# Pairing heads 4 to 7 as (5,4) and (7,6) from the second group on

## The chip, the cores and the metric

The kernel runs on one core of a Trainium2 chip. A core has five engines that run their own instruction streams side by side: PE (TensorE, matrix products; its weight loads are listed apart as PEld), DVE (VectorE), ACT (ScalarE), POOL (GpSimd) and SP (SyncE, which here only issues DMA transfers). Data moves between DRAM and the on-chip memory by 16 DMA engines; a transfer is issued by an instruction on SP, ACT or POOL and lands later. The on-chip memory has 128 partitions; a tile lies across them, and an instruction works on all the partitions of a tile, or on a part of them, at once.

The metric is the device time of one execution in microseconds (us). The kernel before takes 655.81 us, the median of 3 runs (653.32 to 656.08).

## The reference

An attention with decay over 4 batches, 8 heads, 768 positions and head size 64, whose output, with heads side by side, is the 3072x512 input x of two matrix products with a pointwise function between them:

```python
q, k, v: (4, 8, 768, 64) float32; lam: (8,) in 0.97 to 0.99
w_in: (512, 2048); w_out: (2048, 512)          # both float64
for b in range(nb):                            # blocks of 64 positions
    qb, kb, vb = (q[:, :, sl], k[:, :, sl], v[:, :, sl])
    intra = np.einsum('bhic,bhjc->bhij', qb, kb) * Dmask[None]
    intra = np.einsum('bhij,bhjd->bhid', intra, vb)
    inter = np.einsum('bhid,bhde->bhie', qb * lam_pow[None], kv_state)
    out[:, :, sl] = intra + inter
    kv_state = lam_block * kv_state + einsum(kb * rev_pow, vb)
x = np.ascontiguousarray(out.transpose(0, 2, 1, 3)).reshape(B * S, H * D)
h = x @ w_in
g = h - np.tanh(h)
return (g @ w_out).astype(np.float32)
```

The row index of w_in is head times 64 plus the place in the head. The order in which the kernel keeps the 512 values of a token is therefore free, as long as the rows of w_in are in the same order.

## The kernel before

**Tiling.** The kernel takes blocks of 128 positions. A group g (0 to 5) is one such block of all 4 batches: 512 tokens, of which half 0 is batches 0 and 1 (P0) and half 1 batches 2 and 3 (P1). For each group the attention gives x transposed (`xt`: 4 chunks of 128 rows, 256 tokens a half), the first product gives the hidden values, the second the output. Products after group 0 are made by sums and seven products of half size in place of eight (`up`, L640), the second product from group 1 on by two levels of this (`down_twice`, L932). The summed blocks of w_out lie in DRAM (`fine`) and are fetched again for every group through POOL's queue into a ring of seven buffers named `wb` (L814). A matmul that finds its `wb` block not landed waits.

**Heads in pairs.** The 8 heads are handled as four pairs p of two heads j, one in partitions 0 to 63 and one in 64 to 127. Before, pair p holds heads 2p and 2p+1 in this order. The scores of a pair are masked by powers of lam (`mask0` in group 0, `mask` from group 1 on, both made at the start), and the state is kept in `state`, two heads of a pair one below the other. `fwd` (`powers`) holds lam's powers for q, one row per place in the pair.

**x is written in a swapped order.** From group 1 on a tile of scores is shared by the pairs p and p+2, pair p with one half of the positions in the upper rows and pair p+2 with the other, and `out_banks` puts the output of pairs 2 and 3 into the opposite half of the partitions (`1 - j`). So the rows of x come as heads 0, 1, 2, 3, 5, 4, 7, 6. w_in must be in the same order: its blocks m = 0 and 1 of a unit (512 columns; there are four units) come in one transfer to 128 partitions each, the blocks m = 2 and 3 in two transfers to 64 partitions each, to swapped halves (`load_block`, L238). The raw 64-bit weights are rounded to float32 by three ACT copies (L318 to L320) and two DVE operations (L322, L323) a block, with four raw buffers (`WAHEAD`), so that block n+4 is not issued until block n has been rounded.

**Loads of q, k and v.** Everything here is issued by SP in the order in which the program states it. In groups 0 and 1, q and k come in natural layout (L156), are transposed on PE (L374) and copied out of PSUM by ACT (`att_transpose`, L376, one copy of 128x512 for q and one for k). From group 2 on, q and k come as blocks: `load_blocks` fetches them, one tile for q and one for k of each batch, with four transfers a tile (L174), each to 32 partitions with pieces of up to 1 KB for four heads; DVE then turns the tile in 32x32 squares (L352). The natural k and v (L161, three transfers each) are needed as well, for the state and the output. `load(n)` is called by the first user of a group's blocks and issues the whole group from group 2 on: k and v of batches, the blocks of batches 0 to 3, and the natural k and v that remain; a block's transfer must wait until the tile that it goes into has been turned. SP's transfers use eight completion semaphores in turn, and an issue waits until the transfer eight before it has landed.

**Order at the start.** SP issues q, k and v of batches 0 and 1, then q and k of batch 2, w_in blocks 0 and 1, q and k of batch 3, w_in block 2, v of batches 2 and 3, and w_in block 3. PE does group 0's attention for batches 0 and 1, begins the first product of unit 0 (`up_plain`, L1012) between the parts for batches 2 and 3, whose `state_products` (L421) needs their v, and then goes on with w_in block by block. Group 1's transposes follow while the rest of the weights arrives.

**Order later.** Tile's scheduler places what isn't tied (`keep_in_program_order`); matmuls of the attention for the next group are put between the products of the current one. `out_late` (L508) and `out_early` (L522) multiply v with the masked scores, `score_products` (L458) k with q. `copy_xt` (L412) brings x out of PSUM.

Of the kernel before, what the change touches and what calls it, by code (L numbers as in the profile page):

```python
# [24 lines left out]
def kernel(  # L25
# [79 lines left out]

    mask = const.tile([128, 4, 3, HF], F32)

    def masks():
        inj = work.tile([128, BLK], F32, name="inj", tag="qd")
        cross = work.tile([128, 4, 2, HF], F32, name="cross", tag="qd")  # L110
        lo, hi = ts(0, HF), ts(1, HF)
        nc.gpsimd.memset(inj[hi, HF:BLK], 0.0)
        nc.gpsimd.tensor_copy(inj[hi, 0:HF], ident[hi, HF:BLK])
        for n in range(4):
            tc.keep_in_program_order(nc.vector.tensor_tensor_scan(
                out=cross[hi, n].rearrange("s c i -> s (c i)"), data0=lam_all[hi, n + 4:n + 5].to_broadcast([HF, BLK]),
                data1=inj[hi], initial=0.0, op0=AL.mult, op1=AL.add))
        m0 = mask0.rearrange("s j p (c i) -> s p j c i", c=2)
        for q in range(2):
            n = ts(q, 2)  # L120
            nc.gpsimd.tensor_copy(mask[lo, n, 0:2], m0[lo, q])
            nc.gpsimd.tensor_copy(mask[lo, n, 2], m0[lo, q + 2, :, 0])
            nc.gpsimd.tensor_copy(mask[hi, n, 1], m0[hi, q, :, 1])
        nc.gpsimd.tensor_copy(mask[hi, :, 0:3:2], cross[hi])

    fwd = const.tile([128, NP, BLK], F32)

    def powers():
        for j in range(2):
            tc.keep_in_program_order(nc.vector.tensor_copy(  # L130
                fwd[ts(j, 64), :, 0], lam_all.rearrange("s (p j) -> s j p", j=2)[ts(j, 64), j, :]))
        m = 1
        while m < BLK:
            tc.keep_in_program_order(nc.vector.tensor_tensor(
                fwd[:, :, m:2 * m], fwd[:, :, 0:m], fwd[:, :, m - 1:m].to_broadcast([128, NP, m]), op=AL.mult))
            m *= 2
# [3 lines left out]
    bwd = [mask[:, :, c, HF - 1:HF].to_broadcast([128, H // 2, D]) for c in (1, 2)]  # L140
# [23 lines left out]
    def load_blocks(g, b, names):  # L164


        for name, src in (("q", q), ("k", k)):
            if name in names:
                x = late["blk"].tile([128, NP, 4 * D], F32, name=f"{name}_blk", tag="blk")
                for c in range(4):  # L170
                    n = 4 * D - 32 * (c % 2)
                    at_ = src[b, c // 2, g * BLK, 32 * (c % 2):]
                    rows = bass.AP(tensor=at_.tensor, offset=at_.offset, ap=[[4 * D, 32], [2 * S * D, NP], [1, n]])
                    tc.keep_in_program_order(nc.sync.dma_start(out=x[ts(c, 32), :, 0:n], in_=rows))  # L174
# [55 lines left out]
    def load_block(eng, dst, kind, n, m, first=False):  # L230
# [3 lines left out]
        elif m < 2:  # L234
            tied(first, eng.dma_start(out=dst, in_=w_in_u[ts(m, 128), n]))
        else:
            for j in range(2):
                tied(first, eng.dma_start(out=dst[ts(1 - j, 64)], in_=w_in_u[ts(2 * m + j, 64), n]))  # L238
# [123 lines left out]
    def att_transpose(g, bs):  # L362
        for b in bs:
# [4 lines left out]
            for dst, x in ((qt, "q"), (kt, "k")):  # L368
                if g >= GB:
                    turn_block(dst, t[x + "b"])  # L370
                else:
# [4 lines left out]
                    tied(True, nc.scalar.activation(dst, tp, AF.Copy))  # L376
# [28 lines left out]
    def out_banks():  # L405
        ops = [bank("op", "att", 4).rearrange("d (p b s) -> d p b s", p=2, b=2) for _ in range(2)]
        return ops, lambda n, p, j: ops[p // 2][ts(j if p < 2 else 1 - j, 64), p % 2, n, :]
# [7 lines left out]
    def state_products(g, bs, kv):  # L415
        kv = kv.rearrange("d (b p e) -> d b p e", b=2, p=NP)
        for n, b in enumerate(bs):
            kd, vn = raw[g, b]["k"], raw[g, b]["v"]
            for p in range(NP):
                for j in range(2):  # L420
                    tied(True, nc.tensor.matmul(out=kv[ts(j, 64), n, p, :], lhsT=kd[:, 2 * p + j, :],  # L421
                                                rhs=vn[:, 2 * p + j, :], start=n == 0 and p == 0, stop=True,
# [7 lines left out]
    def first_out(bs):  # L430
        ops, dst = out_banks()
# [51 lines left out]
    def att_read(g, bs):  # L483
        half = bs[0] // 2
        begun = (g, half) in outs
        if not begun:
            outs[g, half] = out_banks()
# [12 lines left out]
    def out_late(g, bs, first=False):  # L500
        if first:
            outs[g, bs[0] // 2] = out_banks()
        _, dst = outs[g, bs[0] // 2]
        for n, b in enumerate(bs):
            ss, vn = sc[g, b], raw[g, b]["v"]
            for p in range(NP):
                for j in range(2):
                    tied(True, nc.tensor.matmul(out=dst(n, p, j)[:, HF:BLK], lhsT=vn[:, 2 * p + j, :],  # L508
# [4 lines left out]
    def out_early(g, bs):  # L513
        ops, dst = outs.pop((g, bs[0] // 2))
        behind = seen.pop((g, bs[0] // 2), None)
        for n, b in enumerate(bs):
            ss, vn = sc.pop((g, b)), raw[g, b]["v"]
            for q in range(2):
                for p in (q, q + 2):
                    for j in range(2):  # L520
                        r = ts(p // 2, HF)
                        mm = tied(True, nc.tensor.matmul(out=dst(n, p, j)[:, 0:HF], lhsT=vn[r, 2 * p + j, :],  # L522
# [836 lines left out]
```

## Time and profile before

| | us |
|---|---|
| median of 3 runs | 655.81 (653.32 to 656.08) |
| the profiled execution | 655.09 |
| its span | 653.3 |
| granted PE clock | 1.000 |
| DVE, ACT, POOL busy | 494.7, 241.1, 231.0 |
| moved by DMA | 140.45 MB, mean 215 GB/s |
| SP's and ACT's transfers (hardware queues) | 28.0% of 16 engines' span |
| POOL's transfers (software queue) | 46.9% of it |

The span goes from the first instruction that is recorded to the last; the time of the execution holds 1.8 us besides. The two largest groups of POOL's transfers are the `wb` fetches and the writes of `fine`:

```profile
L814 POOL DMA_DIRECT2D wb<-fine x217 | 116.7, 539 | 219.8 <-PE y L932 110.5 <-PE y L867 38.5 <-PE zw L932 30.8
L305 POOL DMA_DIRECT2D fine<-f x32 | 20.9, 658 | 3.6 <-DMA fine<-f 1.4 <-DVE ws L323 0.9 <-DVE ws L285 0.4
```

A line of this kind reads: source line, engine, operation, what it writes and reads, how many; then the busy time in us and the mean in ns of one; then the idle time of that engine just before them and what ended most of it. The groups that turn the q and k blocks, on DVE:

```profile
L352 DVE STREAM_TRANSPOSE kt<-k_blk 128x512 f32<-128x512 f32 x16 | 17.8, 1110 | 0.0
L352 DVE STREAM_TRANSPOSE qt<-q_blk 128x512 f32<-128x512 f32 x16 | 17.7, 1107 | 0.0
```

The share of DMA in a row of windows is that of the busy time of 16 engines, and it may be above 1 where records overlap. In a row in order of time the first number is the time from the span's start, the second the length, and a bracket holds the idle time before and what ended it.

### The profile page before, as it was taken

What the parts mean: (1) busy time and instruction counts of PE and PEld (TensorE: products, weight loads), DVE (VectorE), ACT (ScalarE), POOL (GpSimd) and SP (SyncE); (2) the same over time, 40 slices, a digit from 0 to 9 for tenths busy, and PEclk for the clock granted to TensorE, in tenths of its full rate; (3) what the DMA queues carried; (4) which work ended last, traced back from release to release, by engine and by line L of the source; (5) the groups of instructions that cost most, each with busy time, mean ns of one, the idle gap of its engine ahead of it and who ended that gap; (6) DMA issues with size and microseconds to landing.
All of it is one profiled execution on the core that took longest, in us unless ns stands there. A gap on an engine that the chain in (4) does not pass through costs nothing.

```text
span 653.3 us, 14777 instructions
## 1 busy us (share of the span) xinstructions
PE 639.9 (98%) x5792; PEld 589.3 (90%) x5792; DVE 494.7 (76%) x884; ACT 241.1 (37%) x484; POOL 231.0 (35%) x396
## 2 busy tenths in 40 slices
PE   7899999999999999999999999999999999999998
PEld 6688888888888999988999988999988999988997
DVE  4798997996876976898768777878777878256583
ACT  3788682603321223442122453222344212444110
POOL 2120247773113554243455100546201356300450
PEclk9999999999999999999999999999999999999999
DMA  9979978999458876999978775779693587610582
GB/s 215 223 204 187 281 235 296 327 317 290 114 157 221 261 228 221 250 286 239 296 244 287 202 145 130 234 241 303 200 195 98 161 290 252 213 39 0 158 280 80
DMA packets 108261, 140.45 MB, mean 215 GB/s; under 512 B 64032, under 2 KB 81568, under 8 KB 108192
## 3 DMA queue, kind: packets, MB, share of 16 engines
q0 software_dynamic: 29840, 97.54, 46.9%
q1 hardware_dynamic: 78208, 41.96, 28.0%
q8 instruction: 46, 0.75, 0.5%
q14 instruction: 23, 0.19, 0.1%
q10 hardware_dynamic: 144, 0.00, 0.0%
HBM read 117.18 MB, written 23.86 MB: 216 GB/s over the span
## 4 chain that ended last, share of the span: by engine, by line
PE 72%; DMA 4%; DVE 3%; issue 3%; POOL 2%; ACT 1%; POOLq 0%; DVEq 0%; ACTq 0%
PE y L640 17%; PE y L932 14%; PE zw L932 11%; PE z L640 6%; PE w L640 5%; PE y L738 4%; DMA wb<-fine 3%; PE z L738 2%; PE acc L1042 2%; PE y L867 2%; PE sp L458 2%; DMA fine<-f 1%; PE op L508 1%; POOL wb L814 1%; PE op L494 1%
## 5 line engine op out<-in xcount | busy, mean ns | idle before, releaser
L814 POOL DMA_DIRECT2D wb<-fine x217 | 116.7, 539 | 219.8 <-PE y L932 110.5
L932 PE MATMUL y<-wb,g 128*128 128x128 f32 x624 | 81.4, 276 | 1.3 <-DMA wb<-fine 1.3
L935 ACT ACTIVATE q<-y 128x128 f32<-128x128 f32 x108 | 29.9, 277 | 137.9 <-PE y L932 137.9
L932 PEld LDWEIGHTS y<-wb,g 128*128 128x128 f32 x624 | 75.3, 192 | 2.3 <-DVE q L890 1.4
L932 PE MATMUL zw<-wb,g 128*128 128x128 f32 x416 | 55.3, 276 | 0.8 <-DMA wb<-fine 0.7
L932 PEld LDWEIGHTS zw<-wb,g 128*128 128x128 f32 x416 | 50.6, 192 | 1.3 <-issue 0.5
L640 PE MATMUL y<-xt,w 128*128 128x256 f32 x200 | 46.9, 380 | 0.0
L648 ACT ACTIVATE th<-g 128x512 f32<-128x512 f32 x42 | 26.5, 630 | 51.9 <-DVE g L671 20.0
L1012 PE MATMUL h<-xt,w 128*128 128x256 f32 x192 | 44.2, 382 | 1.0 <-DVE w L323 1.0
L653 DVE TENSOR_TENSOR g<-g,th 128x512 f32<-128x512 f32 x42 | 29.1, 692 | 17.4 <-ACT th L648 17.2
L640 PEld LDWEIGHTS y<-xt,w 128*128 128x128 f32 x200 | 37.6, 190 | 5.1 <-ACT g L680 0.2
L1012 PEld LDWEIGHTS h<-xt,w 128*128 128x128 f32 x192 | 35.7, 190 | 6.4 <-DVE w L323 0.9
L640 PE MATMUL w<-xt,w 128*128 128x256 f32 x168 | 40.4, 382 | 0.0
L640 PE MATMUL z<-xt,ws 128*128 128x256 f32 x168 | 39.7, 379 | 0.0
L640 PE MATMUL y<-tt,w 128*128 128x256 f32 x160 | 38.1, 381 | 0.0
L640 PE MATMUL y<-tt,ws 128*128 128x256 f32 x160 | 38.1, 380 | 0.0
L640 PEld LDWEIGHTS z<-xt,ws 128*128 128x128 f32 x168 | 31.9, 190 | 4.3
L640 PEld LDWEIGHTS w<-xt,w 128*128 128x128 f32 x168 | 31.0, 190 | 4.5 <-ACT w L611 0.4
L640 PEld LDWEIGHTS y<-tt,w 128*128 128x128 f32 x160 | 30.1, 190 | 4.3
L932 PE MATMUL y<-wb,s 128*128 128x128 f32 x248 | 32.8, 275 | 1.0 <-DMA wb<-fine 1.0
L640 PEld LDWEIGHTS y<-tt,ws 128*128 128x128 f32 x160 | 30.0, 190 | 3.9
L932 PE MATMUL zw<-wb,s 128*128 128x128 f32 x248 | 32.8, 275 | 0.0
(216 smaller groups left out, 1373.9 us busy)
## 6 DMA issues: line engine op xcount, KB each, us to landing
wb<-fine POOLq DMA_DIRECT2D x217, 256.0 KB, 3.8
fine<-f POOLq DMA_DIRECT2D x24, 256.0 KB, 4.9
wb<-fine_in POOLq DMA_DIRECT2D x24, 256.0 KB, 4.3
raw<-in_moe_w_out_dram POOLq DMA_DIRECT2D x10, 512.0 KB, 6.6
raw<-in_moe_w_in_dram SPq DMA_DIRECT2D x8, 512.0 KB, 5.2
raw<-in_moe_w_in_dram SPq DMA_DIRECT2D x16, 256.0 KB, 6.0
q_blk<-in_q_dram SPq DMA_DIRECT2D x32, 128.0 KB, 4.2
k_blk<-in_k_dram SPq DMA_DIRECT2D x32, 128.0 KB, 5.0
```

The source lines that it names most:

```text
L458: tied(True, nc.tensor.matmul(out=dst, lhsT=keys(p, j, late_), rhs=qt[ts(j, 64), p, rows], start=True, stop=True))
L494: tied(True, nc.tensor.matmul(out=dst(n, pp, j), lhsT=state[r, b, pp, :], rhs=tr[g, b][2][r, pp, :], start=not begun and n == 0 and p == 0 ...
L640: tied(g == 0, nc.tensor.matmul(out=t[:, m, :], lhsT=wt[:, kt, ts(m, 128)], rhs=x[:, kt, :], start=first and m == 0 and kt == 0, stop=kt = ...
L648: tied(g == 0, nc.scalar.activation(th, src, AF.Tanh))
L653: tied(g == 0 or g >= GI and inside, nc.vector.tensor_tensor(dst(c), src, th, op=AL.subtract))
L738: tied(True, nc.tensor.matmul(out=dst[:, ts(u, 128)], lhsT=a, rhs=b, start=x in (1, 2, 5) and u == 0, stop=True, skip_group_check=True))
L814: nc.gpsimd.dma_start(out=t.rearrange("p m c -> p (m c)"), in_=fine[TWICE.index(n_), SLOT.index(x_)].rearrange("p u c -> p (u c)"))
L867: nc.tensor.matmul(out=t[:, m, :], lhsT=a[:, u, kt, ts(m, 128)], rhs=wb[:, kt, :], start=first and u == 0 and m == 0 and kt == 0, stop=u = ...
L932: tied(True, nc.tensor.matmul(out=dst, lhsT=a[:, u, :], rhs=wb[:, ts(u, 128)], start=x in begins and u == 0, stop=u == NU - 1, skip_group_ ...
L935: nc.scalar.activation(keep, dst, AF.Copy)
L1012: tied(u == 0 or u == 2 and cs[0] == 11, nc.tensor.matmul(out=hm[c][:, m, :], lhsT=w1[u][:, i, a, ts(m, 128)], rhs=xt[0, t][:, i, :], star ...
L1042: nc.tensor.matmul(out=acc[n][:, r, :], lhsT=a[:, ts(r, 128)], rhs=b, start=kt == 0 and r == 0, stop=kt == KH - 1, skip_group_check=True)
```

## The change

A function `head(p, j)` names the head in place j of pair p: as before for pairs 0 and 1, and swapped, (5,4) and (7,6), for pairs 2 and 3. Because `out_banks` swaps those pairs again, x comes in natural order. Group 0 keeps natural pairs in its scores and writes its output unswapped (`out_banks(0)`), while its state products already use the swapped pairing. All that reads or writes a head by its pair follows: `powers` (four copies in place of two), `masks` (two copies more on POOL, and two into the new constant `fall`, which holds the decay of the lower half and which DVE's decay now reads in place of a slice of the mask), the slices of k and v in `state_products`, `out_late` and `out_early`. In group 1, whose transposes on PE are as before, ACT's copy out of PSUM is made as three: pairs 0 and 1 at once, and two of 64 partitions that swap the halves of pairs 2 and 3. The q and k blocks from group 2 on, whose transfers took four heads at a constant step, now take two heads each, so a tile has eight transfers in place of four. Every w_in block is one transfer.

Instructions on each engine, before and after, without the semaphore and register kinds: PE 2930 and 2930, in the same sequence; DVE 886 and 888; ACT 487 and 503; POOL 401 and 405; SP 290 and 410.

```diff
+    def head(p, j):
+        return 2 * p + (j if p < 2 else 1 - j)
...
     mask = const.tile([128, 4, 3, HF], F32)
+    fall = const.tile([128, 4], F32)
...
         for n in range(4):
+            h = head(n // 2 + 2, n % 2)
             tc.keep_in_program_order(nc.vector.tensor_tensor_scan(
-                out=cross[hi, n].rearrange("s c i -> s (c i)"), data0=lam_all[hi, n + 4:n + 5].to_broadcast([HF, BLK]),
+                out=cross[hi, n].rearrange("s c i -> s (c i)"), data0=lam_all[hi, h:h + 1].to_broadcast([HF, BLK]),
                 data1=inj[hi], initial=0.0, op0=AL.mult, op1=AL.add))
...
             nc.gpsimd.tensor_copy(mask[lo, n, 0:2], m0[lo, q])
-            nc.gpsimd.tensor_copy(mask[lo, n, 2], m0[lo, q + 2, :, 0])
+            for j in range(2):
+                nc.gpsimd.tensor_copy(mask[lo, 2 * q + j, 2], m0[lo, q + 2, 1 - j, 0])
             nc.gpsimd.tensor_copy(mask[hi, n, 1], m0[hi, q, :, 1])
         nc.gpsimd.tensor_copy(mask[hi, :, 0:3:2], cross[hi])
+        for j in range(2):
+            nc.gpsimd.tensor_copy(fall[:, j::2], mask[:, 1 - j::2, 2, HF - 1])
...
         for j in range(2):
-            tc.keep_in_program_order(nc.vector.tensor_copy(
-                fwd[ts(j, 64), :, 0], lam_all.rearrange("s (p j) -> s j p", j=2)[ts(j, 64), j, :]))
+            for p in (0, 2):
+                h = head(p, j)
+                tc.keep_in_program_order(nc.vector.tensor_copy(
+                    fwd[ts(j, 64), p:p + 2, 0], lam_all[ts(j, 64), h:h + 3:2]))
         m = 1
...
     bwd0 = mask0.rearrange("s j p i -> s p j i")[:, :, :, BLK - 1:BLK].to_broadcast([128, NP, 2, D])
-    bwd = [mask[:, :, c, HF - 1:HF].to_broadcast([128, H // 2, D]) for c in (1, 2)]
+    bwd = [x.to_broadcast([128, H // 2, D]) for x in (mask[:, :, 1, HF - 1:HF], fall[:, :, None])]
...
                     n = 4 * D - 32 * (c % 2)
-                    at_ = src[b, c // 2, g * BLK, 32 * (c % 2):]
-                    rows = bass.AP(tensor=at_.tensor, offset=at_.offset, ap=[[4 * D, 32], [2 * S * D, NP], [1, n]])
-                    tc.keep_in_program_order(nc.sync.dma_start(out=x[ts(c, 32), :, 0:n], in_=rows))
+                    for p in (0, 2):
+                        at_ = src[b, head(p, c // 2), g * BLK, 32 * (c % 2):]
+                        rows = bass.AP(tensor=at_.tensor, offset=at_.offset, ap=[[4 * D, 32], [2 * S * D, 2], [1, n]])
+                        tc.keep_in_program_order(nc.sync.dma_start(out=x[ts(c, 32), p:p + 2, 0:n], in_=rows))
                 raw[g, b][name + "b"] = x
...
             tied(n > 4, eng.dma_start(out=dst, in_=moe_w_out[ts(2 * (n + m) - n % 2, 128), :].rearrange("k (a n) -> k a n", a=2)))
-        elif m < 2:
+        else:
             tied(first, eng.dma_start(out=dst, in_=w_in_u[ts(m, 128), n]))
-        else:
-            for j in range(2):
-                tied(first, eng.dma_start(out=dst[ts(1 - j, 64)], in_=w_in_u[ts(2 * m + j, 64), n]))
...
                                                                    identity=ident))
-                    tied(True, nc.scalar.activation(dst, tp, AF.Copy))
+                    if g == 0:
+                        tied(True, nc.scalar.activation(dst, tp, AF.Copy))
+                        continue
+                    tied(True, nc.scalar.activation(dst[:, 0:2], tp[:, 0:2], AF.Copy))
+                    for j in range(2):
+                        tied(True, nc.scalar.activation(dst[ts(j, 64), 2:4], tp[ts(1 - j, 64), 2:4], AF.Copy))
             tr[g, b] = [qt, kt, None]
...
-    def out_banks():
+    def out_banks(g):
         ops = [bank("op", "att", 4).rearrange("d (p b s) -> d p b s", p=2, b=2) for _ in range(2)]
-        return ops, lambda n, p, j: ops[p // 2][ts(j if p < 2 else 1 - j, 64), p % 2, n, :]
+        return ops, lambda n, p, j: ops[p // 2][ts(j if p < 2 or g == 0 else 1 - j, 64), p % 2, n, :]
...
                 for j in range(2):
-                    tied(True, nc.tensor.matmul(out=kv[ts(j, 64), n, p, :], lhsT=kd[:, 2 * p + j, :],
-                                                rhs=vn[:, 2 * p + j, :], start=n == 0 and p == 0, stop=True,
+                    tied(True, nc.tensor.matmul(out=kv[ts(j, 64), n, p, :], lhsT=kd[:, head(p, j), :],
+                                                rhs=vn[:, head(p, j), :], start=n == 0 and p == 0, stop=True,
                                                 skip_group_check=True))
...
     def first_out(bs):
-        ops, dst = out_banks()
+        ops, dst = out_banks(0)
         for n, b in enumerate(bs):
...
         if not begun:
-            outs[g, half] = out_banks()
+            outs[g, half] = out_banks(g)
         ops, dst = outs[g, half]
...
         if first:
-            outs[g, bs[0] // 2] = out_banks()
+            outs[g, bs[0] // 2] = out_banks(g)
         _, dst = outs[g, bs[0] // 2]
...
                 for j in range(2):
-                    tied(True, nc.tensor.matmul(out=dst(n, p, j)[:, HF:BLK], lhsT=vn[:, 2 * p + j, :],
+                    tied(True, nc.tensor.matmul(out=dst(n, p, j)[:, HF:BLK], lhsT=vn[:, head(p, j), :],
                                                 rhs=ss[:, j, p % 2, 1 + p // 2, :], start=first and n == 0 and p % 2 == 0,
...
                         r = ts(p // 2, HF)
-                        mm = tied(True, nc.tensor.matmul(out=dst(n, p, j)[:, 0:HF], lhsT=vn[r, 2 * p + j, :],
+                        mm = tied(True, nc.tensor.matmul(out=dst(n, p, j)[:, 0:HF], lhsT=vn[r, head(p, j), :],
                                                          rhs=ss[r, j, q, 0, :], start=False, stop=True,
```

## The prediction

> **What bounds the kernel now.** I read the busy shares first, then busy time by ten-microsecond window, then the order of time on PE, SP and ACT in the windows where PE is not full, and last the landing of single transfers. First the page's busy line and the chain that ended last:
>
> ```profile
> PE 639.9 (98%) x5792; PEld 589.3 (90%) x5792; DVE 494.7 (76%) x884; ACT 241.1 (37%) x484; POOL 231.0 (35%) x396
> ...
> PE 72%; DMA 4%; DVE 3%; issue 3%; POOL 2%; ACT 1%; POOLq 0%; DVEq 0%; ACTq 0%
> ```
>
> PE is busy for 639.9 of 653.3 us. All that any change of transfers and copies can win is therefore the 13.4 us in which PE idles. The windows (columns: window, its length, busy PE, PEld, DVE, ACT, POOL with counts, clock, DMA share, GB/s) say where these are:
>
> ```profile
> 10.00:20.00 10.00, 8.82 (x121) 7.63 (x121) 5.46 (x11) 7.06 (x13) 0.00 (x0) 1.00 1.18 260
> 20.00:30.00 10.00, 8.57 (x100) 7.07 (x99) 7.34 (x21) 5.57 (x10) 0.58 (x1) 1.00 1.05 237
> 30.00:40.00 10.00, 9.51 (x44) 8.05 (x43) 8.83 (x11) 8.97 (x16) 6.34 (x5) 1.00 0.78 218
> 300.00:310.00 10.00, 9.05 (x120) 8.58 (x112) 9.11 (x17) 2.79 (x7) 4.29 (x8) 1.00 1.02 244
> 310.00:320.00 10.00, 8.39 (x71) 8.10 (x72) 6.40 (x10) 1.39 (x5) 4.00 (x8) 1.00 0.92 304
> ```
>
> Some 5.9 us are lost before 40 us, 2.6 us in 300 to 320, about 1.6 us in four small places between 110 and 230, and 3 us behind the last matmul. Everywhere else PE is full, at clock 1.00. Of the early loss, these three waits stand behind a w_in block (PE in order of time):
>
> ```profile
> 24.16 0.69 PE L421 MATMUL kv<-v_nat,k_nat 128*64 128x64 f32 x16 [0.23 <-DMA v_nat<-in_v_dram]
> 26.04 0.69 PE L421 MATMUL kv<-v_nat,k_nat 128*64 128x64 f32 x16 [1.19 <-DMA v_nat<-in_v_dram]
> 30.89 8.04 PE L1012 MATMUL h<-xt,w 128*128 128x256 f32 x36 [0.49 <-DVE w L323]
> ```
>
> Together 1.91 us. The other early waits are for the first q, k and POOL's identity, ahead of any block that changes.
>
> **Part 1, w_in blocks in one transfer.** Eight blocks (m of 2 and 3, four units) lose one of two issues each, 8 issues of some 0.59 us in all. The issues cost nothing by themselves: SP has slack. What counts is how fast the bytes land, since DMA is full here (share 1.05 to 1.18) and v_nat of batches 2 and 3 stands behind block 2:
>
> ```profile
> 12.21 4.08 SPq L238 DMA_DIRECT2D raw<-in_moe_w_in_dram  x2
> 16.34 1.21 SPq L156 DMA_DIRECT2D v_nat<-in_v_dram  x2
> 17.59 5.28 SPq L238 DMA_DIRECT2D raw<-in_moe_w_in_dram  x2
> ```
>
> Windows of one microsecond, in the same columns, show the rate while a whole block lands (13 to 14) and while the two halves of block 2 land (20 to 23):
>
> ```profile
> 13.00:14.00 1.00, 1.00 (x22) 0.93 (x19) 0.69 (x2) 0.51 (x1) 0.00 (x0) 1.00 1.00 401
> 20.00:21.00 1.00, 1.00 (x7) 0.59 (x7) 1.00 (x2) 0.79 (x2) 0.00 (x0) 1.00 1.27 124
> 22.00:23.00 1.00, 1.00 (x7) 0.90 (x6) 0.96 (x2) 0.00 (x0) 0.00 (x0) 1.00 0.94 155
> ```
>
> Landing by landing: whole blocks 0 and 1 land 1.28 and 1.39 us behind what went before; the pair of block 2 takes 3.79 us (19.26 to 23.05), the pair of block 3 1.80 us (25.91 to 27.71). So one block saves between 0.5 us (1.80 - 1.3) and 2.5 us (3.79 - 1.3). With 1.5 us, the middle, v_nat of batch 3 lands at 24.4 instead of 25.91 and block 3 two savings earlier: all three waits close. With 0.5 us about 1.0 of the 1.91 us close. I take 1.7 us of gain, bounds 1.0 and 1.9. It carries on because behind 30.89 PE, ACT and DVE wait for each other and no longer for w_in (PE is 10.00 of 10 us from 40 to 110).
>
> **Part 2, ACT's copies in group 1.** Eight copies of 128x512 (600 ns each, L376) become one 128x256 and two 64x256 each, 16 instructions more. No 256-wide copy is in the trace; between 277 ns (128x128, L935) and 600 ns it comes to 385 ns, 1155 for three. By durations that is +0.56 us a tile, 4.4 us in all; by the start-to-start step of copies in a row (0.48 against 0.60 us, so 0.12 overlaps) +0.3 us a tile, 2.5 us in all. They lie at 59.8, 70.6 and 74.9 us, and ACT then waits anyway (idle in the brackets):
>
> ```profile
> 70.12 0.60 ACT L1019 ACTIVATE th<-h 128x512 f32<-128x512 f32 x1 [1.72 <-PE h L1012]
> 74.89 0.60 ACT L376 ACTIVATE qt<-tp 128x512 f32<-128x512 f32 x1 [1.33 <-PE tp L374]
> 81.89 1.08 ACT L412 ACTIVATE xt<-op 128x512 f32<-128x512 f32 x2 [2.51 <-PE op L522]
> ```
>
> Queued behind the copies are the w_out conversions, which DVE's L323 waits for; DVE slips by some 0.7 us at 73 and 78 us and regains it in its own waits for ACT (0.35 at 84.86, 0.41 at 86.66). PE needs the results of this stretch from 93.6 us on. Price 0; without that cover, up to 1.3 us.
>
> **Part 3, small work.** Two more copies of `powers` on DVE (the two there take 0.34 us together) and four on POOL (64x64 and 128x2; the row for 64x64 is 0.23 us) lie before 30.4 us; POOL's sums end at 36.5 and PE reads them from 43.16. PE's matmuls keep number, order and shape, only slices change; DVE's decay reads `fall` instead of the mask. Price 0, at most 0.3 us.
>
> **Part 4, the q and k blocks in twice the transfers.** 128 issues become 256 of half the size: each group from 2 on has 8 tiles (q and k of four batches), and a tile has 8 issues instead of 4. One issue lasts 0.43 us (median of L174), so a tile takes SP 3.4 us instead of 1.7. SP also uses eight completion semaphores in turn: the second piece of q for batch 3 is issued at 267.69, right when the eighth before it (261.26, landing 6.4 us later) has landed. Eight in flight are now one tile, not two. Behind the blocks on SP stand the natural k and v:
>
> ```profile
> 265.12 4.04 SPq L174 DMA_DIRECT2D q_blk<-in_q_dram  x4
> ...
> 273.44 5.17 SPq L161 DMA_DIRECT2D k_nat<-in_k_dram  x3
> ...
> 282.77 2.33 SPq L161 DMA_DIRECT2D v_nat<-in_v_dram  x3
> ```
>
> The last piece of v for batch 1 lands at 291.2; PE needs it at 296.9 (L508), 295.2 with the gain of part 1. From 260.9 on, four tiles take four rounds of landing time L; then 12 issues of 0.62 us and a landing of about 4 us: in time while 260.9 + 4L + 11.4 < 295.2, L < 5.7 us. Before, with twice the bytes in flight, L was 6.4 to 9.7 us for most of these; DMA is full there (share 1.12), so with half the bytes in flight I take about half, 4.1 to 4.5: no wait. The blocks' own users (DVE L352) have more: q of batch 2 lands by some 269 and is turned at 273.4. Groups 4 and 5 have L of 3 to 5.6 and 5 us or more to spare. In group 2 each tile's issue waits for a DVE turn every 5.5 us: hidden.
>
> Behind that, blocks for group 4 are issued from about 298 us to 314 instead of 296.7 to 306.5. At 310.3, 311.8 and 313.9 PE waits 1.28, 0.31 and 0.96 us for wb; these transfers share DMA with the blocks (12 pieces, 1.4 MB, land from 304 to 314). At 0.47 us an issue the halves bring 1.2 MB in that time: -0.3 us, bounds -2.5 (stall gone) and +1.5 (it moves behind 314). In group 4 the same overlap arises for the first time, from 409.8, when wb starts again (needed 4.9 us after issue, 2.9 to 3.5 now): +0.2, bounds 0 and 1.
>
> A rule of the Trainium skill speaks against part 4: the page "DMA: Bandwidth & Descriptors", section "Measured", puts a 64 KB transfer at 0.95 us and calls smaller ones descriptor-dominated. By it, as an estimate, 32 halves would take 30 us and v would be late by about 7.5 us, some 661.5 us in all. The trace does not bear it out: 64 KB pieces of v (388.7 to 389.7 us) land 0.4 to 0.5 us apart.
>
> **Sum.** -1.7 + 0 + 0 + (-0.3 + 0.2) = -1.8 us. The profiled execution took 655.09 us (653.3 span, 1.8 around it), which gives 653.3; the median of the runs, 655.81, lies 0.7 us above it, so 654.0.
>
> **Rivals.** (A) The forecast: 654.0, own range 652.5 to 655.6.
> (B) Slower: v_nat of group 3 comes late. It decides from L = 5.7 us. If a half keeps 7.2 us (landing set by POOL's traffic, not by SP's own bytes in flight), v is 4 x 1.5 = 6 us late at L508, a full PE stall: 660.0. For it: the first block at 260.9 took 4.2 us with nothing of SP's ahead, the second 6.4. Against: that traffic eases by 294 (share 0.89).
> (C) Faster: the wb stall at 310 goes as well, since SP feeds its blocks more thinly: 655.81 - 1.7 - 2.55 = 651.6. For it: DMA share 1.04 to 1.13 from 304 to 314. Against: the blocks come later and so stay longer.
> (D) Whole blocks land no earlier, the 124 GB/s at 20 us being DMA's mix and not the halves: 655.8. Against it: 401 GB/s at 13 us at the same share.
>
> **How the numbers follow.** A 0.52, B 0.15, C 0.22, D 0.11. What a measurement here can tell from no change is 0.5%, 3.3 us: below 652.5 and above 659.1. Faster: C and the edge of A, 0.25; slower: B, 0.15; same: 0.60. The range runs from 651.2 to 658.3: A, D, most of C and the mild part of B.
>
> **What would show it.** Right: no v_nat wait at L421 near 24 to 26 us; block 2 landing 1.3 us behind k; PE some 1.7 us earlier at 40 and still at 290; L508 of group 3 unwaited. Wrong: a DMA wait at L508 or L458 near 295, block landings over 5.7 us, longer wb waits at 310 or 410, or ACT's copies delaying L1042.

## The result, and the profile after

The changed kernel takes 661.44 us (median of 7 runs, 658.11 to 662.49) where the kernel before takes 653.35 (7 runs, 652.86 to 656.97). The ratio is 1.0101, with a 95% interval of 1.0074 to 1.0127: 1% slower, 6.6 us by the ratio, where 1.8 us faster (654.0), with a range up to 658.3, had been forecast. Beside the last experiments the changed kernel was run again: 659.57 us, ratio 1.0071 (1.0046 to 1.0096). The profiled execution of the first seven took 658.11 us, the shortest of them, with a span of 656.3, 3.0 us more than that of before.

The page's busy line and the chain that ended last:

```profile
PE 642.1 (98%) x5792; PEld 590.2 (90%) x5792; DVE 494.4 (75%) x886; ACT 245.6 (37%) x500; POOL 232.3 (35%) x400
...
PE 68%; DMA 6%; SPq 4%; DVE 3%; issue 2%; POOL 2%; ACT 1%; DVEq 0%; POOLq 0%; ACTq 0%
```

PE's sequence of matmuls has not changed, and yet PE counts as busy for 2.2 us longer. SPq, SP's own issuing, stands in the chain with 4%; before it was not there. The windows of the changed kernel, in the columns used in the prediction:

```profile
10.00:20.00 10.00, 8.81 (x121) 7.73 (x122) 5.41 (x11) 7.01 (x13) 0.00 (x0) 1.00 1.17 289
20.00:30.00 10.00, 8.94 (x101) 7.15 (x101) 8.58 (x24) 7.70 (x14) 1.66 (x3) 1.00 0.83 268
30.00:40.00 10.00, 10.00 (x48) 8.79 (x47) 9.15 (x13) 7.25 (x13) 6.04 (x5) 1.00 0.70 218
...
300.00:310.00 10.00, 9.44 (x83) 9.21 (x81) 8.36 (x15) 1.99 (x6) 5.37 (x10) 1.00 0.88 248
310.00:320.00 10.00, 7.90 (x61) 7.07 (x60) 6.22 (x11) 1.39 (x5) 3.80 (x8) 1.00 1.06 286
320.00:330.00 10.00, 9.54 (x79) 8.89 (x78) 8.09 (x12) 1.39 (x5) 5.04 (x10) 1.00 0.98 301
400.00:410.00 10.00, 10.00 (x197) 9.09 (x196) 6.84 (x11) 3.39 (x7) 0.48 (x1) 1.00 0.46 122
410.00:420.00 10.00, 8.66 (x74) 8.11 (x72) 8.76 (x14) 1.39 (x5) 5.43 (x11) 1.00 0.95 239
```

Up to 40 us PE idles less than before, from 310 on more, and at 410 there is a hole that was not there. Before, these were the rows for 400 to 420 us:

```profile
400.00:410.00 10.00, 10.00 (x195) 9.06 (x194) 6.89 (x11) 3.39 (x7) 0.24 (x1) 1.00 0.24 47
410.00:420.00 10.00, 10.00 (x92) 10.00 (x91) 8.55 (x14) 1.66 (x6) 6.08 (x12) 1.00 0.76 248
```

Since both kernels run the same 5,792 matmuls in the same order, the sharpest view is to take the start of each matmul in the one trace from its start in the other (negative: the changed kernel is ahead):

| at (time in before) | changed minus before, us | step |
|---|---|---|
| 24 | -0.2 | |
| 26 | -1.59 | v of batch 3 is early |
| 31 to 114 | -1.14 | 0.45 given back at once |
| 117 to 230 | -1.6 to -2.4 | three small waits gone or shorter |
| 310 to 314 | -4.8 | before's own wb stall of 2.55 us is gone |
| 314 to 327 | +0.15 | 5.0 lost |
| 416 to 423 | +3.0 | 3.0 lost |
| end | +2.96 | |

So the start gained, and two stretches lost 8 us. PE in order of time in the first of these:

```profile
309.05 1.13 PE L947 MATMUL y<-wb,s 128*128 128x128 f32 x8 [0.56 <-DMA wb<-fine]
310.25 1.16 PE L947 MATMUL zw<-wb,s 128*128 128x128 f32 x8
311.33 1.13 PE L947 MATMUL y<-wb,g 128*128 128x128 f32 x8
314.13 1.13 PE L947 MATMUL zw<-wb,g 128*128 128x128 f32 x8 [1.68 <-DMA wb<-fine]
315.10 1.08 PE L947 MATMUL y<-wb,g 128*128 128x128 f32 x8
316.53 1.16 PE L947 MATMUL y<-wb,gS 128*128 128x128 f32 x8 [0.36 <-DMA wb<-fine]
```

Where wb is on time, eight matmuls start every 0.89 us (before, 315.72, 316.62, 317.51). Here they start 1.0 to 1.2 us apart even where no idle time is shown: the wait lies inside the modelled length of the matmuls. That is where the 2.2 us of "busy" time come from, and the reason why a sum of idle brackets is too small. SP in the same time (SPq: one row for a run of issues, first issue and length):

```profile
295.03 1.98 SPq L173 DMA_DIRECT2D v_nat<-in_v_dram  x3
297.10 4.92 SPq L187 DMA_DIRECT2D q_blk<-in_q_dram  x8
302.12 3.77 SPq L187 DMA_DIRECT2D k_blk<-in_k_dram  x8
305.98 5.71 SPq L187 DMA_DIRECT2D q_blk<-in_q_dram  x8
313.47 7.71 SPq L187 DMA_DIRECT2D k_blk<-in_k_dram  x8
```

The four tiles for group 4 need 24 us on SP (9.7 before) and land until 326.6 us (313.9 before), while wb is being fetched from 301.6 us on. One group later:

```profile
380.04 3.68 SPq L187 DMA_DIRECT2D k_blk<-in_k_dram  x8
383.82 1.70 SPq L173 DMA_DIRECT2D k_nat<-in_k_dram  x3
...
397.27 1.91 SPq L173 DMA_DIRECT2D v_nat<-in_v_dram  x3
399.28 3.83 SPq L187 DMA_DIRECT2D q_blk<-in_q_dram  x8
...
413.18 5.44 SPq L187 DMA_DIRECT2D k_blk<-in_k_dram  x8
```

Before, SP's rows for the tiles of group 5 were these:

```profile
391.92 1.97 SPq L174 DMA_DIRECT2D q_blk<-in_q_dram  x4
393.98 1.80 SPq L174 DMA_DIRECT2D k_blk<-in_k_dram  x4
395.88 1.81 SPq L174 DMA_DIRECT2D q_blk<-in_q_dram  x4
397.79 1.80 SPq L174 DMA_DIRECT2D k_blk<-in_k_dram  x4
```

The last of these issues was at 399.15, and all had landed at 403.1, 6.7 us before wb started at 409.8. Now SP issues almost without a pause, 7.4 us later at 399.28 because the blocks ahead of the natural loads took that much longer, and the last half lands at 426.5. Meanwhile DMA has room: its share from 400 to 410 us is 0.46. What the blocks queue for there is SP, not DMA. This is the second meaning that the Trainium skill's page "Perfetto Trace Analysis", section "What "DMA-bound" means", gives to the word: the issuing sequencer's track is solid with DMA slices. The trace agrees, with the numbers just shown.

### The profile page after: what moved, and what is told of

Read it like the earlier page. It is cut to its first block, busy times and chain, and to the rows that moved or that the text cites. A ratio compares the mean times of both kernels' runs of the same rounds, so it can differ in the third digit from the quotient of the medians.

```text
span 656.3 us, 14982 instructions
## 1 busy us (share of the span) xinstructions
PE 642.1 (98%) x5792; PEld 590.2 (90%) x5792; DVE 494.4 (75%) x886; ACT 245.6 (37%) x500; POOL 232.3 (35%) x400
## 4 chain that ended last, share of the span: by engine, by line
PE 68%; DMA 6%; SPq 4%; DVE 3%; issue 2%; POOL 2%; ACT 1%; DVEq 0%; POOLq 0%; ACTq 0%
PE y L947 15%; PE y L655 14%; PE zw L947 11%; PE z L655 5%; PE w L655 5%; PE y L753 4%; SPq L187 4%; DMA wb<-fine 2%; PE y L882 2%; PE z L753 2%; PE acc L1057 2%; PE sp L473 2%; DMA k_blk<-in_k_dram 2%; PE op L523 1%; PE op L509 1%
```

## The experiments

All are compared with the kernel before on the same chip, in five rounds. The theory after the result: SP's issue, which costs 0.43 us for a half block as for a whole one, brings the blocks too late, so that they move beside wb.

**One part alone: halves.** In the kernel before:

```diff
-                    rows = bass.AP(tensor=at_.tensor, offset=at_.offset, ap=[[4 * D, 32], [2 * S * D, NP], [1, n]])
-                    tc.keep_in_program_order(nc.sync.dma_start(out=x[ts(c, 32), :, 0:n], in_=rows))
+                    for p in (0, 2):
+                        at_ = src[b, 2 * p + c // 2, g * BLK, 32 * (c % 2):]
+                        rows = bass.AP(tensor=at_.tensor, offset=at_.offset, ap=[[4 * D, 32], [2 * S * D, 2], [1, n]])
+                        tc.keep_in_program_order(nc.sync.dma_start(out=x[ts(c, 32), p:p + 2, 0:n], in_=rows))
```

> The kernel before with one part of the change alone: each q and k block transfer of four heads is made as two of two heads (same heads, same order; 128 issues more on SP). Theory (late blocks): SP needs 0.43 us an issue whatever the size, so the blocks of the next group are still landing when the w_out blocks (wb) start at about 304 and 410 us, and PE waits for wb. In the two profiles this cost 2.5 us between 311 and 327 us and 3.0 us between 416 and 423 us. Expected here: 5 to 9 us slower than before, with the wb waits at those two places. Rival (the loss is in ACT's split copies, the masks or POOL's small work): within 1 us of before.

Measured: 660.99 us against 655.36, ratio 1.0102 (1.0082 to 1.0122). The halves alone make the whole loss. Against the trace of before, matmul by matmul, 6.5 us are lost between 314 and 328 (2.6 of them had just been gained on before's own stall) and 2.5 between 415 and 423.

**The same issues, blocks whole.** In the kernel before a transfer of 4 bytes stands behind each whole block:

```diff
                     tc.keep_in_program_order(nc.sync.dma_start(out=x[ts(c, 32), :, 0:n], in_=rows))
+                    tc.keep_in_program_order(nc.sync.dma_start(
+                        out=spare[:, at["spare"]:at["spare"] + 1],
+                        in_=bass.AP(tensor=lam.tensor, offset=lam.offset, ap=[[1, 1], [1, 1]])))
+                    at["spare"] += 1
```

> The kernel before, q and k blocks whole, with a transfer of 4 bytes from lam to an unused place in DRAM issued on SP behind each block transfer. The issues are 128 more and at most four blocks are in flight, as with halves, but each block is still 128 KB in one transfer. Theory (SP's issues and the eight in flight set the pace): the same loss as with halves, 5 to 9 us. Rival (a half-sized transfer is itself moved less well by the DMA engines): within 1 us of before.

Measured: 665.9 us, ratio 1.0176 (1.0153 to 1.0199). More than forecast: a small issue took 0.56 us, so a block and its companion take 1.0 us of SP where two halves take 0.9. v for group 3 came late as well, and there are losses near 217, 297 and 403 us besides those at 313 to 333. Part of PE's order also moved in this build, so the size is not to be compared closely. But the rival falls: a block of full size loses as much when SP is as busy.

**One part alone: w_in.** The kernel before with the one transfer for all blocks, so that the rows of heads 4 to 7 do not meet x:

```diff
-        elif m < 2:
+        else:
             tied(first, eng.dma_start(out=dst, in_=w_in_u[ts(m, 128), n]))
-        else:
-            for j in range(2):
-                tied(first, eng.dma_start(out=dst[ts(1 - j, 64)], in_=w_in_u[ts(2 * m + j, 64), n]))
```

> The kernel before with every w_in block in one transfer to 128 partitions and nothing else, so the rows of w_in for heads 4 to 7 do not meet their rows of x. Theory (the start gains what the trace of the changed kernel shows): 1.1 us earlier at 40 us, 1.9 us at 130 us, and in all 1 to 2.5 us faster than before. Rival (whole blocks bring nothing that lasts): within 0.5 us of before.

Measured: 653.52 us against 655.36, ratio 0.9984 (0.9963 to 1.0006), about 1 us, not clear of nothing. In the seven profiles with whole w_in blocks and DVE's order untouched, PE stands at 40 us between -1.13 and -1.40 us against the trace of before (mean -1.21); in six others with w_in in halves between -1.00 and +1.22 (mean -0.47, five of them below -0.5). So 0.4 to 0.8 us of the 1.14 are the change's, and the rest was the one execution that had been profiled.

**One part alone: ACT's copies**, without the swap of halves:

```diff
-                    tied(True, nc.scalar.activation(dst, tp, AF.Copy))
+                    if g == 0:
+                        tied(True, nc.scalar.activation(dst, tp, AF.Copy))
+                        continue
+                    tied(True, nc.scalar.activation(dst[:, 0:2], tp[:, 0:2], AF.Copy))
+                    for j in range(2):
+                        tied(True, nc.scalar.activation(dst[ts(j, 64), 2:4], tp[ts(j, 64), 2:4], AF.Copy))
```

> The kernel before with each of ACT's eight copies of group 1's transposes made as one of 128x256 and two of 64x256, without the swap of halves (the result is the same). Theory (hidden): within 0.5 us of before. Rival (the copies push back the weights' rounding and cost PE time from 85 us on): 1.3 us or more slower.

Measured: 654.39 us, ratio 0.9988 (0.9972 to 1.0004): no cost.

**Less for SP to issue, with halves and without.** The natural loads (three transfers each) made one, in the changed kernel and in the one before:

```diff
-                if name == "q" or g == 0:
+                if True:
                     tc.keep_in_program_order(
                         nc.sync.dma_start(out=x, in_=src[b, :, ts(g, BLK), :].rearrange("h s d -> s h d")))
```

> The changed kernel with each natural k and v load of a group from 1 on as one transfer in place of three (the same bytes in the same pieces of 256 bytes; the two halves of 64 positions of heads 4 to 7 then keep their order, so the output differs). SP issues 16 transfers fewer a group. Theory (SP's time is the pace): per group the issues for q, k and v take SP about 64 x 0.43 + 8 x 0.62 = 32.5 us, where the changed kernel takes 64 x 0.43 + 24 x 0.62 = 42.4 and the kernel before 32 x 0.43 + 24 x 0.62 = 28.6. So most of the loss goes: between 1.5 us faster and 2.5 us slower than before. Rival (half-sized blocks are moved less well, whenever they are issued): still 5 us or more slower than before.

> The kernel before with the natural k and v loads as one transfer in place of three (the halves of 64 positions of heads 4 to 7 keep their order, so the output differs), blocks whole. SP needs 32 x 0.43 + 8 x 0.62 = 18.7 us a group for q, k and v in place of 28.6. Theory (SP's time is the pace): the blocks for group 4 land before wb starts, and the 2.55 us of wb wait between 310 and 314 us shrink or go: 1 to 3 us faster. Rival (that wait is DMA's own, whatever SP does): within 0.5 us of before.

Measured: the changed kernel 655.62 us against 654.52, ratio 1.0018 (1.0002 to 1.0034); the kernel before 652.76, ratio 0.9976 (0.9958 to 0.9994). The halves are still there, each issued and moved as in the changed kernel, and most of the 1.0% has gone; the rival for it, 5 us or more, falls. Not all of their cost is gone: between these two kernels, alike but for the change, there are still 2.9 us. With whole blocks the wb stall of before shrinks to one short wait:

```profile
311.41 1.13 PE L932 MATMUL y<-wb,s 128*128 128x128 f32 x8 [0.52 <-DMA wb<-fine]
```

**The law of it.** For each trace I counted the bytes of q and k blocks whose packets started later than 1.5 us after the first wb issue of the stretch, and took the time of the same 300 matmuls (in before from 300.42 to 332.80 us, and from 406.02 to 435.65):

| kernel | MB of blocks beside wb, group 3 | us | group 4, MB | us |
|---|---|---|---|---|
| before, natural loads whole | 0.01 | 29.87 | 0 | 29.36 |
| before | 0.58 | 32.38 | 0 | 29.63 |
| w_in alone | 0.66 | 32.15 | 0 | 29.72 |
| changed, natural loads whole | 1.23 | 34.19 | 0 | 29.35 |
| changed | 1.48 | 34.88 | 0.85 | 32.70 |
| halves alone | 1.65 | 36.28 | 0.74 | 32.25 |
| changed, second profile | 1.84 | 36.18 | 0.75 | 31.94 |

From 0.01 to 1.84 MB the time grows by 6.31 us, 3.45 us for each MB, which is 290 GB/s. That is DMA's rate there (286 and 301 GB/s in the windows above), and also what wb needs: 256 KB every 0.89 us is 295 GB/s. While PE eats wb at full pace, DMA has little to spare (its share is 0.88 at 290 GB/s from 320 to 330 us in the kernel before with natural loads whole, and 1.06 and 0.98 in the two windows above), and a byte of a block pushes wb back by about its own time. Small amounts cost nothing that shows: with 0.12 and 0.20 MB in group 4 (the two runs below of the changed kernel with v moved) the 300 matmuls took 29.2 us.

In the table the rows with much of group 3's blocks beside wb are all halves, so it can't part the size of a transfer from the time at which it moves. Two other traces can. In the changed kernel with v on POOL, further below, PE came to this stretch so late, for another reason, that all halves had moved before: 0 MB and 29.78 us, as with whole blocks. In the run with small transfers between whole blocks it was 1.41 MB and 35.12 us (with a few matmuls in another order). Halves or not does not matter here; when they move does. The traces that are not in the table lie within 1 us of the same line, but for one (before with v later, 0 MB and 32.47 us), where the clock stood at 0.50 from 308 to 312 us.

**A way around the halves.** The kernel before with w_in whole, its pairing and its blocks kept, group 0's output unswapped, and the swap put into ACT's copy of x (shown in part):

```diff
...
         for c in range(2):
-            tied(g < GB, nc.scalar.activation(x[:, 2 * c:2 * c + 2, :].rearrange("d p (b s) -> d p b s", b=2), ops[c],
-                                              AF.Copy))
+            y = x[:, 2 * c:2 * c + 2, :].rearrange("d p (b s) -> d p b s", b=2)
+            if c == 0 or g == 0:
+                tied(g < GB, nc.scalar.activation(y, ops[c], AF.Copy))
+                continue
+            for j in range(2):
+                tied(g < GB, nc.scalar.activation(y[ts(j, 64)], ops[c][ts(1 - j, 64)], AF.Copy))
...
```

> The kernel before with the pairing kept, every w_in block one transfer, group 0's output unswapped, and ACT's copy of x for pairs 2 and 3 from group 1 on made as two of 64 partitions that swap the halves (L412; 10 copies more in the whole kernel). No block is split. Theory: the start gains as in the run with w_in alone, ACT has room: 0.5 to 2 us faster than before. Rival (the longer copy, about 0.5 us each, stands between the attention and the first product and delays the sums of x): 1 us or more slower.

Measured: 656.39 us, ratio 1.0023 (1.0004 to 1.0043), 1.5 us slower: the rival. DVE, in order of time, waits for the longer copy before it can make the sums of x:

```profile
335.50 0.69 DVE L580 TENSOR_TENSOR tt<-xt,xt 128x512 f32<-128x512 f32 x1 [3.50 <-ACT xt L411]
336.72 0.69 DVE L581 TENSOR_TENSOR tt<-xt,tt 128x512 f32<-128x512 f32 x1 [0.53 <-ACT xt L414]
```

and ACT's next copy of a product (L936), which stands behind the copies of x, comes late for the matmul at 337.04. This step of 0.49 us recurs near 214, 236, 335, 438 and 540 us; 0.9 us more went at 116 us in a wait for DVE.

**PE's next wait at the start.** The same kernel with powers and masks moved:

```diff
     weights(3)
-    powers()
-    masks()
     first_state(P1)
     weights(KI)
+    powers()
...
     weights(KI + 1)
+    masks()
```

> The same, and powers moved behind the rounding of w_in block 3 and masks behind that of block 4 in DVE's and POOL's order. Theory (once v is early, PE's next wait, 0.99 us at 29.75 us in the changed kernel, is for a w_in block whose rounding stands behind 3.7 us of powers and masks on DVE): that wait goes and PE at 40 us is 0.5 to 1 us earlier than without the move. Rival (ACT's part of the rounding is late by itself, or the work moved delays the next block by as much): no difference at 40 us.

Measured: 656.94 us, ratio 1.0041 (1.0023 to 1.0058), no faster than without the move. PE in this kernel:

```profile
26.69 9.76 PE L1013 MATMUL h<-xt,w 128*128 128x256 f32 x44
...
40.78 1.56 PE L641 MATMUL w<-xt,w 128*128 128x256 f32 x6 [1.23 <-DVE w L320]
```

The wait near 29 us is gone and PE is 2.48 us ahead of before at 40 us (1.28 without the move), but it waits for the rounding of a later w_in block at 40.78 and is 0.74 us ahead at 45. Both sides of the expectation were half right: the wait was DVE's order, and DVE, with the same work in another order, is late one step on.

**Part of SP's work given to POOL.** The 12 natural v loads of groups 3 to 5:

```diff
...
-            nat = "kv" if g < NG - 1 else "v"
+            nat = "kv" if g == GB else "k" if g < NG - 1 else ""
...
-            table["end"] = [(att_end, h), (att_qd, k, P0)]
+            table["end"] = [(att_end, h), (load_v, k), (att_qd, k, P0)]
...
+    def load_v(g):
+        for b in range(B):
+            load_natural(g, b, "v", nc.gpsimd)
```

> The kernel before with the 12 natural v loads of groups 3, 4 and 5 issued by POOL right behind the state products of the group before, in place of SP; the result is the same. SP's time for q, k and v falls from 28.6 to 32 x 0.43 + 12 x 0.62 = 21.2 us a group. Theory (SP's time is the pace): the wb wait at 310 us shrinks, 0.5 to 2 us faster. Rival (POOL's own queue: its wb and fine transfers stand behind 12 more issues): 1 us or more slower.

> The changed kernel with the same move; the result is the same. SP's time falls from 42.4 to 64 x 0.43 + 12 x 0.62 = 35.0 us a group, between the kernel before (28.6) and the changed one, and near the run with natural loads whole (32.5, which was 0.2% slower than before). Theory: 0 to 4 us slower than before, at least 3 us better than the changed kernel. Rival (the half blocks' bytes beside wb cost the time, however early the rest is): still 6 us slower than before.

> The changed kernel itself once more, beside the others on one chip, and a second profile of it: its profiled execution was the fastest of seven. Theory: 1.0% slower than before; a typical execution has the same two places of wb waits as the first profile, each longer. Rival (a typical execution loses somewhere else as well): its extra time lies in other places.

Measured: before with the move 662.92 us against 654.84, ratio 1.0128 (1.0106 to 1.0151); changed with the move 658.2, 1.0059 (1.0038 to 1.008); the changed kernel again 1.0071. The first is the rival, at one place that I had not foreseen. The second is 1.4 us better than the changed kernel beside it, where at least 3 had been expected, for the same reason. DVE and PE in the kernel before with the move:

```profile
285.39 0.69 DVE L895 TENSOR_TENSOR f<-f,f 128x512 f32<-128x512 f32 x1 [10.20 <-DMA f<-factors]
...
290.86 3.78 PE L645 MATMUL y<-tt,w 128*128 128x256 f32 x8 [10.10 <-DVE g L667]
```

In group 2 alone, POOL also fetches factors for DVE, and these now stood behind v. (The clock was 0.50 from 290 to 296 us, so that the eight matmuls took 3.78 us, not 1.89.) Behind that wait, between 300 and 333 us, both kernels are faster than before (by 1.8 and 2.6 us). The second profile of the changed kernel loses in the two known places and nowhere else: 3.8 us from 300 to 333, 2.3 from 406 to 436, and ends at +4.43 us.

**The same with group 3's v loads behind seven of the factors' transfers**, in `later_units`:

```diff
+                if (g, u) == (GI, 0):
+                    load_v(g + 1)
```

> The kernel before with the v loads of groups 3 to 5 on POOL as before, but those of group 3 behind the first seven transfers of factors in POOL's queue; the result is the same. Theory (SP's time is the pace): no wait of DVE for factors near 282 us, a shorter wb wait at 310, 0.5 to 2 us faster than before. Rival (POOL's queue is as full as SP's): the wait at 282 stays or turns up at another place, slower than before.

> The changed kernel with that move; the result is the same. In the run with v on POOL the delta to before went from +6.6 us at 285 to +4.6 us at the end, so without the new wait at 282 it would end about 3 us ahead of before by the trace. Theory (all of the loss is SP's time): between 2.5 us faster and 0.5 us slower than before. Rival (half blocks beside wb cost the time whatever SP does): 3 us or more slower than before.

Measured: before with this 660.75 us, ratio 1.0088 (1.0061 to 1.0115): the same wait at another place, DVE idle for 7.21 us up to 300.14 for the second set of factors. The changed kernel with this: 654.82 us against 653.75, ratio 1.0012 (0.9994 to 1.0029), 0.8 us slower, which lies nearer the theory than the rival. The loss of 0.7 to 1.0% comes down to 0.1% although every half transfer is still there: SP's lateness was what the halves cost. Its trace still loses 1.6 us near 288 us, most of it in a wait for DVE, and 2.0 us from 300 to 333, part of it to the clock (last section). It does not beat the kernel before. The only run that is clearly faster, before with natural loads whole, keeps the two halves of the positions of heads 4 to 7 in the other order and so computes something else.

## Why the prediction was wrong

**The step that failed is in part 4: the price of the overlap with wb.** It saw all the pieces: an issue takes SP 0.43 us at half the size too, eight in flight are one tile, the blocks of group 4 come later and share DMA with wb. It priced the overlap at -0.3 us for group 3 (bounds -2.5 and +1.5) and +0.2 for group 4 (0 to 1). In the two profiles of the changed kernel the same 300 matmuls took 2.5 and 3.8 us longer in group 3, and 3.1 and 2.3 us longer in group 4; the halves alone cost 1.02%, 6.7 us. Two errors lie in that term. The forecast reckoned that halves "bring 1.2 MB in that time", and so that thinner feeding relieves wb. From 304 to 314 us they did bring less (0.73 MB against 0.89), but the rest came behind that. It should have asked how many bytes are moved before wb starts: from 297 to 304 us whole blocks bring 1.07 MB, halves 0.49 (packets counted in the two traces), and DMA is half idle instead (share 0.48 from 300 to 302). What misses that time must run beside wb, at 3.45 us an MB. And the delay adds up: SP is one queue, and the 7.4 us by which it was late at 399 are not in the price for group 4, which names an overlap from 409.8 us but no lateness of SP.

**Rival B** was nearest in size (660.0), but not where it put the loss: the last piece of v for batch 1 landed at 293.5 us and the matmul that reads it ran at 294.53 without a wait. The margin was 1.0 us. The landing time of halves, which B feared at 7.2 us and the forecast put at 4.1 to 4.5, was 4 to 6 us for the first two tiles and then 2 to 4; the four tiles took 18.8 us, 4.7 each. Beside wb in group 3 it was 6 to 9.7 us, which fits B's reason, that others' traffic sets it, but no run shows that by itself.

**Rival C**, that the stall at 310 us goes, did happen in its own place (309 to 314 us, 2.5 us gained) and was paid back within 15 us. In the kernel before with natural loads whole it nearly held (one wait of 0.52 us is left), by the opposite means: more done before wb, not less at once.

**Part 1** was right in kind and too large: 1.7 us forecast, bounds 1.0 and 1.9; about 1 us by its own run, not clear of nothing, and 0.4 to 0.8 us over all profiles. v of batch 3 landed at 22.87 where I expected 24.4, and the two v waits closed. The third wait did not. PE in the changed kernel:

```profile
23.93 1.15 PE L436 MATMUL kv<-v_nat,k_nat 128*64 128x64 f32 x32
...
29.75 3.50 PE L1027 MATMUL h<-xt,w 128*128 128x256 f32 x15 [0.99 <-DVE w L333]
```

The 0.49 us wait for a rounded block grew to 0.99, since powers and masks, 3.7 us of DVE, stand ahead of it. "PE, ACT and DVE wait for each other" was true, and I had not gone on to ask which of them is late next. And part of the wait priced was chance: block 2's halves took 3.79 us from what went before in that execution, 2.6 and 2.7 in two other runs with halves. Whole, it took 2.47 us in the changed kernel, not the 1.3 that the prediction took over from blocks 0 and 1; more of the gain was in the v behind it. **Rival D**, that whole blocks land no earlier, falls as to the landing: v of batch 3 landed from 22.6 to 23.0 us in the eight profiles with whole blocks, and from 24.8 to 26.3 in six with halves.

**Part 2** was right as a price of nothing, and the copies took a little more than estimated. ACT in the changed kernel:

```profile
69.79 0.41 ACT L389 ACTIVATE qt<-tp 128x256 f32<-128x256 f32 x1
70.21 0.77 ACT L391 ACTIVATE qt<-tp 64x256 f32<-64x256 f32 x2
...
80.74 1.08 ACT L427 ACTIVATE xt<-op 128x512 f32<-128x512 f32 x2 [1.41 <-PE op L537]
```

A tile takes 1.2 us where its one copy took 0.6, so 0.6 more against 0.3 to 0.56 estimated, and the cover was there: ACT still waits for PE at 80.74, and PE's lead stays at -1.14 from 31 to 114 us. **Part 3** cost nothing that shows.

**The rule of the Trainium skill** (page "DMA: Bandwidth & Descriptors", section "Measured"), 0.95 us for a 64 KB transfer, gave 661.5 us in the prediction's estimate. That is close to what was measured, but it stood for a wait (v late by 7.5 us) that did not arise, so that its nearness, like that of rival B, is luck. The trace does not agree with 0.95 us for halves that come one behind the other: from 400 to 409 us, away from wb, they land 0.5 us apart, about as fast as SP issues them.

What stays open is how much of the lateness is the issue's 0.43 us and how much the limit of eight in flight. The trace shows the first from 399 to 409 us (most issues 0.47 us apart, most landing 1.9 us later) and the second from 306 us on (an issue at 309.91 follows the landing at 309.89 of the transfer eight before it). No run parts them.

## What to carry to other kernels

Count a DMA issue as time on its queue, over the whole span between two busy stretches of DMA, and carry the delay on to the next stretch: twice the issues for the same blocks moved 0.6 MB out of a time in which DMA was half idle into one in which it was full. Where a stream that PE consumes uses nearly all that DMA moves there (here 295 of some 300 GB/s; with another mix, at 13 us, DMA moved 397), other bytes in that time cost about their own transfer time, so the question for any load is first whether it is done before. A gain read from the waits of one profiled execution needs a second execution, and a wait removed needs the name of what PE waits for next.

## What the hardware showed besides

A short stall can cost twice. In the changed kernel with v moved (the last run), PE waited 1.85 us for wb, and a little later the granted clock went to one half. PE in order of time, then windows in the columns used above:

```profile
311.61 1.13 PE L952 MATMUL y<-wb,s 128*128 128x128 f32 x8 [1.85 <-DMA wb<-fine]
312.77 1.69 PE L952 MATMUL zw<-wb,s 128*128 128x128 f32 x8
314.26 1.91 PE L952 MATMUL y<-wb,g 128*128 128x128 f32 x8
315.96 1.38 PE L952 MATMUL zw<-wb,g 128*128 128x128 f32 x8
317.18 1.06 PE L952 MATMUL y<-wb,g 128*128 128x128 f32 x8
```

```profile
312.00:314.00 2.00, 1.97 (x14) 1.78 (x13) 1.97 (x3) 0.28 (x1) 0.54 (x1) 0.81 1.01 273
314.00:316.00 2.00, 2.00 (x12) 2.00 (x11) 0.70 (x2) 0.00 (x0) 0.54 (x1) 0.50 1.07 301
316.00:318.00 2.00, 2.00 (x17) 2.00 (x17) 0.51 (x2) 0.28 (x1) 0.89 (x2) 0.84 1.06 230
```

Eight matmuls take 1.91 us in place of 1.06 until the clock returns, some 2 us lost on top of the wait. In the changed kernel a wait of 1.68 us at 312.5 did not do this, nor did one of 1.94 us, up to 313.55, in the kernel with the swap in ACT's copy and powers moved. But in the kernel before with v later a wait of 1.44 us, up to 26.38 and shortly behind one of 0.35, was enough: the clock was 0.62 and 0.53 in the next two windows of 2 us. The Trainium skill's page "TensorE: Matmul & The Clock Gate", section "Part 1: The HAM clock gate", puts the fall to half clock behind a free-running idle window of about 3.4 us; here 1.44 and 1.85 us without a matmul were enough where 1.94 were not, so the length of the wait alone does not decide it. What does is left open.
